# Softmax of a decode step that takes off each head's maximum: one exp per group of four heads

## The chip, the cores and the metric

The kernel runs on one core of one Trainium2 chip. The metric is the device time of one execution in microseconds (us); the time before is the median of three runs. A profile of one further execution shows each engine's instructions: TensorE (PE; its weight loads are PEld), VectorE (DVE), ScalarE (ACT), GpSimd (POOL) and SyncE (SP), which here only issues transfers and waits.

## The reference, cut to what matters

One token (batch 1, one query) goes through an attention block with a cached K and V and then through a gated MLP. All tensors are bf16. Layer norms have no weights.

```
q  = layernorm(x) @ wq                      # 640 -> 32 heads x 128
s  = q . k_cache * 128**-0.5                # per head 4096 scores
p  = softmax(s)                             # over the 4096 positions
o  = p . v_cache                            # per head 128 values
h  = x + o @ wo                             # 4096 -> 640
y  = layernorm(h)
out = h + (gelu(y @ w_gate) * (y @ w_up)) @ w_down     # 640 -> 1728 -> 640
```

K and V are 33.6 MB each (32 heads x 4096 positions x 128 values). Every byte of them is used once.

## The kernel before, in words

**Groups.** The 32 heads are worked off in 8 groups of four. A group's K (4.2 MB) is one transfer into one of three slots in SBUF, and so is its V. On the partitions, head j of the group has partitions 32j to 32j+31, and each partition holds 128 positions of that head, with their 128 values. The order of the transfers is K0 V0 K1 V1 ... K5 V5 K6 K7 V6 V7; the last V comes in two halves. Transfer n goes into slot n mod 3 and waits until what lay in it has been used: a K slot is free after the last of its four score multiplies, a V slot after its product (`consumed`, line 206). All of them, and the weights, are issued by SP in the order of the program (`issue`, line 197), so a transfer that waits holds up all behind it. After V7 come three parts of wo, which go into the arena that held wq, and then the MLP's weights (lines 462 to 468): two small parts of w_down, w_gate, w_up in two parts, four more parts of w_down. The first of these needs the slot of V7, so it waits for the product of group 7.

**Scores** (`scores`, line 416). A group's scores are made in four steps of 32 positions. DVE multiplies 128x4096 elements of K with the query (L295); PE folds the products eight-fold by matmuls with the identity (L305 and, for the repeated ones, the helper's line L28); DVE sums the remaining 16 (L313) into `sc`. `score_exp` (line 311) then has ACT make the exp of that step's 32 columns in four instructions (L317), one for each head's 32 partitions. Each writes into `p_bd`, in which position g has four columns, one per head: a head's partitions write only their own column, and the rest stays zero from a memset at the start. No maximum is taken off.

**Product with V** (`pv_group`, line 325). For every 8 positions PE takes 32 columns of `p_bd` as weights and multiplies them with two halves of V's 8 positions (L336, and L28 for the repeated weights). The result in `po` holds, beside wanted terms, those of other positions; DVE picks the wanted ones by a mask (`pick`, L353) and sums them (`pick_sum`, L363; for the last two groups three adds, L359 to L361) into `po_r`. PE then sums the 32 partitions of each head (`head_sum`, L369), four groups into one 16-row block of `ps_a`.

**Sums of the probabilities.** `p_sum` (line 348, L349) has DVE sum `p_bd` over the positions; after four groups `z_sum` (line 376) has PE sum over the partitions. `normalize` (line 380) takes the reciprocal and multiplies. `spread` and `take` turn the result into columns for the output projection, `proj_part` (line 395).

**Order.** Every engine works off its list in the order in which the program wrote it; only semaphores join the lists. Within `scores(G)` DVE's order is: multiplies and score sums alternately; before the last score sum the pick of the group whose product was written last (`run(first)`); after it that group's pick sum (`run(later)`); then the row sums of the group before. For K7 no pick is pending, so both lists are empty there. On PE the folds of K7 stand right ahead of the product of group 6.

**The end.** After the product of group 7 (lines 470 to 480): pick, pick sum, first half of the output projection, head sum, normalize, spread, take, second half. Then come the residual and the second layer norm, gate and up matmuls, GELU, the down projection and the output.

Of the kernel before, what the change touches and what calls it, by code (L numbers as in the profile page):

```python
# [17 lines left out]
INV_SQRT_DH = 1.0 / math.sqrt(DH)  # L18
GELU_C0 = math.sqrt(2.0 / math.pi)
GELU_C1 = 0.044715  # L20
NG = 8
# [88 lines left out]
def bass_sequential_preLN__gqa_block_cached__glu_gated_geglu__decode_kernel(nc, A_x, A_k_cache, A_v_cache, A_wq, A_wo, B_x, B_w_gate, B_w_up, B_w_down, out):  # L110
    sb = lambda name, shape, dt: nc.alloc_sbuf_tensor(name, shape, dt)
# [2 lines left out]
    arena = sb("arena", [128, 5 * 4096], BF16)  # L114
    prod = sb("prod", [128, 4, 32, DH], BF16)
    qb = sb("qb", [128, NG, DH], BF16)
    sc = sb("sc", [128, 4, 32], FP32)
    p_bd = sb("p_bd", [128, 2, 128, 4], BF16)
    RT = sb("RT", [128, H], FP32)
# [7 lines left out]
    hlnT = sb("hlnT", [128, 5], BF16)  # L127
    rz = sb("rz", [16, 2], FP32)
    po_m = sb("po_m", [128, 8, DH], FP32)
    po_r = sb("po_r", [128, 2, DH], FP32)  # L130
    m8_t = sb("m8_t", [128, 8, 4, 4], FP32)
    m8 = sb("m8", [128, 8], FP32)
    hs_t = sb("hs_t", [128, 4, 32], FP32)
    hs = sb("hs", [128, 28], FP32)
    aT = sb("aT", [16, 2, 128], BF16)
# [18 lines left out]
    ones_f = sb("ones_f", [128, 128], FP32)  # L154
# [14 lines left out]
    ps_d = bank[4][:, 256:416]  # L169
    ps_s = bank[5]  # L170
    ps_z = bank[6]
    ps_p = bank[7]
# [24 lines left out]
    def issue(upto):  # L197
        while state["next"] < min(upto, len(order)):
# [8 lines left out]
                         for i in range(parts)]  # L207
# [30 lines left out]
    c_par = GP(lambda e: e.affine_select(par_t[:, :, :], ones_b[:, 0:128].rearrange("p (a b) -> p a b", a=2),  # L238
                                         pattern=[[-1, 2], [-2, 64]], compare_op=ALU.is_equal,
                                         fill=0.0, base=0, channel_multiplier=1), c_onesb)  # L240
    c_pbd = GP(lambda e: e.memset(p_bd[:, :, :, :], 0.0))

    c_hs = V(lambda e: e.reduce_sum(hs[:, 12:16], hs_t[:, :, :], axis=AX.X), c_hs, c_hz)
    c_o4 = V(lambda e: e.reduce_max(ones4[:, :], sel4[:, :], axis=AX.X), c_s4)
    c_m8 = V(lambda e: e.reduce_sum(m8[:, :], m8_t[:, :, :, :].rearrange("p a b c -> p a (b c)"), axis=AX.X), c_m8)

    V(lambda e: e.reduce_sum(par[:, :], par_t[:, :, :], axis=AX.X), c_par)


    def x_cols(e):  # L250
# [35 lines left out]
    qc = A(lambda e: e.copy(qb[:, 4:8, :].rearrange("p g d -> p (g d)"), ps_q[1][:, :]), qd)  # L286


    folds, reds, exps, sums, pvs, evs, hds = {}, {}, {}, {}, {}, {}, {}

    def score_mult(s):
        G, n = s // 4, pos[("K", s // 4)]
# [15 lines left out]
            return i  # L308
        folds[s] = T(fold, m, c_idb, reds.get(s - 2))

    def score_exp(s):
        G = s // 4
        reds[s] = V(lambda e: e.reduce_sum(  # L313
            sc[:, s % 4, :], ps_f[s % 2][:, :].rearrange("p (g d) -> p g d", d=16), axis=AX.X),
            folds[s], exps.get(s - 4))
        for j in range(4):
            x = A(lambda e, j=j: e.activation(  # L317
                p_bd[32 * j:32 * j + 32, G % 2, 32 * (s % 4):32 * (s % 4) + 32, j],
                sc[32 * j:32 * j + 32, s % 4, :], ACTF.Exp,
                bias=zero_t[32 * j:32 * j + 32, 0:1], scale=INV_SQRT_DH),  # L320
                reds[s], pvs.get(G - 2), sums.get(G - 2), c_pbd, c_eps)
        exps[s] = x


    def pv_group(G):
        n = pos[("V", G)]
        vt = view(n)
        parts = len(landed[n])

        def pv_mm(e, c, half, load):  # L330
            a = 32 * (c % 4)
            args = (po[a:a + 32, 512 * half:512 * half + 512],
                    p_bd[:, G % 2, 8 * c:8 * c + 8, :].rearrange("p g j -> p (g j)"),
                    vt[:, 8 * c + 4 * half:8 * c + 4 * half + 4, :])
            if load:
                return e.matmul(*args, start=(c < 4), stop=(c >= 12))  # L336
            return matmul_again(nc, *args, c < 4, c >= 12, (128, 32), (0, a))

        for k in range(parts):
            def pv(e, k=k):  # L340
                for c4 in range(4 // parts * k, 4 // parts * (k + 1)):
                    for half in range(2):
                        for c in range(4 * c4, 4 * c4 + 4):
                            i = pv_mm(e, c, half, half == 0)
                return i
            pvs[G] = consumed[n] = T(pv, exps[4 * G + 3], landed[n][k], mks.get(G - 1))

    def p_sum(G):
        sums[G] = V(lambda e: e.reduce_sum(RT[:, 4 * G:4 * G + 4], p_bd[:, G % 2, :, :].rearrange("p g j -> p j g"), axis=AX.X),  # L349
                    exps[4 * G + 3])  # L350

    def pick(G):
        mks[G] = V(lambda e: e.tensor_tensor(  # L353
# [3 lines left out]
    def pick_sum(G):  # L357
        if G >= NG - 2:
            a1 = V(lambda e: e.tensor_add(po_m[:, 0:4, :], po_m[:, 0:4, :], po_m[:, 4:8, :]), mks[G])  # L359
            a2 = V(lambda e: e.tensor_add(po_m[:, 0:2, :], po_m[:, 0:2, :], po_m[:, 2:4, :]), a1)  # L360
            evs[G] = V(lambda e: e.tensor_add(po_r[:, G % 2, :], po_m[:, 0, :], po_m[:, 1, :]), a2, hds.get(G - 2))  # L361
            return
        evs[G] = V(lambda e: e.reduce_sum(po_r[:, G % 2, :], po_m[:, :, :].rearrange("p b d -> p d b"), axis=AX.X),  # L363
                   mks[G], hds.get(G - 2))
# [9 lines left out]
    mks, zs, z4s, spr, aPs = {}, {}, {}, {}, {}  # L374

    def z_sum(t):
        zs[t] = T(lambda e: e.matmul(ps_z[0:16, 0:1], RT[:, 16 * t:16 * t + 16], ones_f[:, 0:1], start=True, stop=True),
                  sums[4 * t + 3], aPs.get(t - 1))
# [49 lines left out]
    headed = 0  # L428
    for kind, G in order:
        if kind == "K":  # L430
            scores(G)
            continue
        run(first)
        run(later)
        pv_group(G)
        while headed in evs:
            head_sum(headed)
            headed += 1
        first.append(lambda G=G: pick(G))
        later.append(lambda G=G: pick_sum(G))  # L440
        if G == 4:
            z_sum(0)
# [159 lines left out]
```

## Time and profile before

| what | us |
|---|---|
| median of 3 runs (203.06 to 203.13) | 203.12 |
| the profiled execution | 202.97 |
| its span | 201.7 |
| DVE busy | 129.5 |
| PE busy | 115.3 |
| ACT busy | 51.3 |
| the costliest group: DVE multiply L295, 32 of 2283 ns | 72.4 |
| ACT exp L317, 128 of 362 ns | 46.4 |
| DVE score sum L313, 32 of 687 ns | 22.0 |
| DVE row sum L349, 8 of 675 ns | 5.4 |

The span is the time from the first to the last recorded instruction; what the device needs ahead of and behind it makes the profiled execution's time. A group line of the profile gives the line of the program, the engine, the operation and the shapes; then its busy time and the mean of one, then the idle time of the engine just before these instructions and what ended it. A line of the timeline gives the start and the length in us, the engine, the instructions merged into it, and in brackets the idle time before it and what ended that.

### The profile page before, as it was taken

The numbers are of one execution on the slowest core, as the hardware profiler recorded it, in microseconds if no ns is written. First come the engines' busy times: TensorE is split into PE (matmuls) and PEld (weight loads), VectorE is DVE, ScalarE is ACT, GpSimd is POOL, SyncE is SP. The second block draws the span as 40 slices with busy tenths as digits, with TensorE's granted clock in tenths as the row PEclk, the third lists the DMA queues.
The fourth block names the chain that finished last, engine by engine and source line by source line (L and its number), as shares of the span: only waits on it lengthen the run. The fifth ranks groups of instructions, "written<-read, shape, count | busy, mean of one in ns | idle before, by whom it ended". The sixth has DMA issues, their size and how long they took to land.

```text
span 201.7 us, 1568 instructions
## 1 busy us (share of the span) xinstructions
PE 115.3 (57%) x788; PEld 17.0 (8%) x384; DVE 129.5 (64%) x136; ACT 51.3 (25%) x139; POOL 5.6 (3%) x15
## 2 busy tenths in 40 slices
PE   0108059536737775197529655876396097754564
PEld 0101000000001000000000001001000000121222
DVE  1300188517994898379857966896879979683341
ACT  2100003610560055005502440252025214500111
POOL 7300000000000000000000000000000000000000
PEclk9999756996996699859997978798569859997575
DMA  9999999999999999999999999999999999999992
GB/s 333 439 398 455 442 422 416 416 442 468 432 422 416 416 422 455 443 442 417 416 416 445 442 448 422 422 416 429 442 442 448 387 429 423 427 409 439 415 408 99
DMA packets 4330, 84.32 MB, mean 418 GB/s; under 512 B 482, under 2 KB 868, under 8 KB 1508
## 3 DMA queue, kind: packets, MB, share of 16 engines
q1 hardware_dynamic: 4322, 84.23, 97.9%
q8 instruction: 4, 0.07, 0.1%
q14 instruction: 2, 0.02, 0.0%
q10 hardware_dynamic: 2, 0.00, 0.0%
HBM read 84.23 MB, written 0.00 MB: 418 GB/s over the span
## 4 chain that ended last, share of the span: by engine, by line
DMA 52%; DVE 21%; PE 19%; issue 3%; ACT 2%; SPq 2%
DMA slot<-in_A_k_cache_dram 43%; DVE prod L295 16%; PE bank L28 13%; DMA slot<-in_B_w_down_dram 9%; DVE sc L313 3%; PE bank L336 3%; PE bank L305 2%; ACT p_bd L317 2%; SPq L59 2%; DVE po_r L363 1%; DVE po_m L353 1%; PE bank L553 0%; DVE out_row L566 0%; DVE RT L349 0%; DVE aP L393 0%
## 5 line engine op out<-in xcount | busy, mean ns | idle before, releaser
L295 DVE TENSOR_TENSOR prod<-slot,qb 128x4096 bf16<-128x4096 bf16 x32 | 72.4, 2283 | 24.3 <-DMA slot<-in_A_k_cache_dram 24.3
L317 ACT ACTIVATE p_bd<-sc,zero_t 32x32 bf16<-32x32 f32 x128 | 46.4, 362 | 107.7 <-DVE sc L313 106.5
L28 PE MATMUL bank<-prod,id_b 128*128 128x512 bf16 x224 | 68.6, 458 | 0.0
L305 PE MATMUL bank<-prod,id_b 128*128 128x512 bf16 x32 | 15.3, 477 | 45.2 <-DVE prod L295 45.1
L313 DVE TENSOR_REDUCE sc<-bank 128x32 f32<-128x512 f32 x32 | 22.0, 687 | 14.7 <-PE bank L28 14.7
L336 PE MATMUL bank<-slot,p_bd 128*32 128x512 bf16 x128 | 14.8, 448 | 15.0 <-ACT p_bd L317 13.8
L28 PE MATMUL bank<-slot,p_bd 128*32 128x512 bf16 x128 | 14.9, 453 | 0.0
L305 PEld LDWEIGHTS bank<-prod,id_b 128*128 128x128 bf16 x32 | 3.5, 109 | 108.6 <-DVE prod L295 108.6
L363 DVE TENSOR_REDUCE po_r<-po_m 128x128 f32<-128x1024 f32 x6 | 11.2, 1867 | 0.0
L353 DVE TENSOR_TENSOR po_m<-bank,m 128x1024 f32<-128x1024 f32 x8 | 9.7, 1214 | 0.6 <-PE bank L28 0.6
L280 PE MATMUL bank<-arena,xlnB 128*32 128x512 bf16 x20 | 3.3, 628 | 7.2 <-DMA arena<-in_A_wq_dram 7.2
L285 DVE CAST qb<-bank 128x512 bf16<-128x512 f32 x1 | 0.7, 692 | 10.0 <-PE bank L28 10.0
L336 PEld LDWEIGHTS bank<-slot,p_bd 128*32 128x32 bf16 x128 | 3.8, 106 | 35.7 <-ACT p_bd L317 26.1
L509 PE MATMUL bank<-slot,hlnT 128*1 128x512 bf16 (+1 forms) x40 | 4.0, 486 | 2.7 <-DVE hX L500 2.2
L349 DVE TENSOR_REDUCE RT<-p_bd 128x4 f32<-128x512 bf16 x8 | 5.4, 675 | 0.0
L252 PE MATMUL bank<-one_bf,x_row 1*128 1x1 bf16 x5 | 0.4, 177 | 7.1 <-DMA x_row<-in_A_x_dram 7.1
L369 PE MATMUL bank<-po_r,hs 128*16 128x128 f32 x16 | 3.4, 301 | 1.5 <-DVE po_r L361 1.5
L286 ACT CAST qb<-bank 128x512 bf16<-128x512 f32 x1 | 0.6, 586 | 10.4 <-PE bank L28 10.4
L28 PE MATMUL bank<-arena,xlnB 128*32 128x512 bf16 x20 | 3.2, 613 | 0.0
L404 PE MATMUL bank<-arena,aP 128*1 128x320 bf16 x32 | 2.5, 314 | 1.1 <-DMA arena<-in_A_wo_dram 1.1
L263 ACT ACTIVATE ln<-ln,eps_t 128x1 f32<-128x1 f32 x2 | 0.6, 294 | 9.4 <-DVE ln L261 9.4
L482 ACT CAST A_hi<-bank 97x320 bf16<-97x320 f32 x1 | 0.4, 426 | 9.8 <-PE bank L28 9.8
(87 smaller groups left out, 42.9 us busy)
## 6 DMA issues: line engine op xcount, KB each, us to landing
slot<-in_A_k_cache_dram SPq DMA_DIRECT2D x8, 4096.0 KB, 21.0
slot<-in_A_v_cache_dram SPq DMA_DIRECT2D x7, 4096.0 KB, 17.7
arena<-in_A_wq_dram SPq DMA_DIRECT2D x1, 5120.0 KB, 15.5
slot<-in_A_v_cache_dram SPq DMA_DIRECT2D x2, 2048.0 KB, 14.9
arena<-in_A_wo_dram SPq DMA_DIRECT2D x1, 2560.0 KB, 22.9
slot<-in_B_w_gate_dram SPq DMA_DIRECT2D x1, 2160.0 KB, 11.0
arena<-in_A_wo_dram SPq DMA_DIRECT2D x1, 1920.0 KB, 27.0
slot<-in_B_w_up_dram SPq DMA_DIRECT2D x1, 1296.0 KB, 13.7
```

Source lines behind the costliest of these rows:

```text
L28: return e.add_instruction(mybir.InstMatmult(name=nc.get_next_instruction_name(), engine=e.engine, start_tensor_calc=start, stop_tensor_ca ...
L59: ev = self.op(eng, lambda e: e.dma_start(out, in_), *deps, dma=True)
L295: m = V(lambda e: e.tensor_tensor(out=prod[:, s % 4, :, :], in0=kt[:, 32 * u:32 * u + 32, :], in1=qb[:, G, :].unsqueeze(1).to_broadcast([1 ...
L305: i = e.matmul(*args, start=True, stop=False)
L313: reds[s] = V(lambda e: e.reduce_sum(sc[:, s % 4, :], ps_f[s % 2][:, :].rearrange("p (g d) -> p g d", d=16), axis=AX.X), folds[s], exps.ge ...
L317: x = A(lambda e, j=j: e.activation(p_bd[32 * j:32 * j + 32, G % 2, 32 * (s % 4):32 * (s % 4) + 32, j], sc[32 * j:32 * j + 32, s % 4, :], ...
L336: return e.matmul(*args, start=(c < 4), stop=(c >= 12))
L349: sums[G] = V(lambda e: e.reduce_sum(RT[:, 4 * G:4 * G + 4], p_bd[:, G % 2, :, :].rearrange("p g j -> p j g"), axis=AX.X), exps[4 * G + 3])
L353: mks[G] = V(lambda e: e.tensor_tensor(out=po_m[:, :, :], in0=po[:, :].rearrange("p (b d) -> p b d", b=8), in1=m8[:, :].unsqueeze(2).to_br ...
L363: evs[G] = V(lambda e: e.reduce_sum(po_r[:, G % 2, :], po_m[:, :, :].rearrange("p b d -> p d b"), axis=AX.X), mks[G], hds.get(G - 2))
L369: return e.matmul(ps_a[0:16, 128 * (G // 4):128 * (G // 4) + 128], hs[:, 12 - 4 * g:28 - 4 * g], po_r[:, G % 2, :], start=(g == 0), stop=( ...
L509: i = e.matmul(po[32 * a:32 * a + 1, 512 * k:512 * k + n], hlnT[:, c:c + 1], w[:, c, 512 * a:512 * a + n], start=(c == 0), stop=(c == 4))
```

## The change

The exp no longer runs step by step. `score_sum` only makes the four score sums, into a doubled `sc`. When a group's last is done, `head_max` takes each partition's maximum (DVE), writes it on the diagonal of 32 columns (ACT, a copy of `d32` with the maximum as scale), and PE multiplies that with `blk`, which is -1/sqrt(128) within each head's 32 partitions and zero elsewhere: 32 columns in which every partition sees the negated, scaled maxima of its head's 32 partitions. `exp_group` takes the minimum of these (DVE), makes one exp of 128x128 with it as the bias (ACT), whose row sums go into an extra column of `po_r`, and spreads the result into `p_bd` by a multiply with the head mask (DVE), zeros included. `pv_group` waits for that spread. The row sums now pass through `head_sum`, which has 129 columns for 128; `p_sum` and `z_sum` are gone, and `normalize` takes its reciprocal from the head sums. `po_r` has four buffers for two. At the start the zeroing of `p_bd` on POOL makes way for one mask there, and two small instructions on DVE are added.

```diff
@@ buffers @@
-    sc = sb("sc", [128, 4, 32], FP32)
+    sc = sb("sc", [128, 2, 4, 32], FP32)
+    mx = sb("mx", [128, NG], FP32)
+    mxd = sb("mxd", [128, 32], FP32)
+    nb = sb("nb", [128, NG], FP32)
+    p_t = sb("p_t", [128, 2, 128], BF16)
...
-    po_r = sb("po_r", [128, 2, DH], FP32)
+    po_r = sb("po_r", [128, 4, DH + 1], FP32)
@@ start @@
-    c_pbd = GP(lambda e: e.memset(p_bd[:, :, :, :], 0.0))
+    c_d32 = GP(lambda e: e.affine_select(d32_t[:, :, :], ones_f[:, :].rearrange("p (a b) -> p a b", a=4),
+                                         pattern=[[-32, 4], [-1, 32]], compare_op=ALU.is_equal,
+                                         fill=0.0, base=0, channel_multiplier=1), c_ones)
...
+    c_d32 = V(lambda e: e.reduce_sum(d32[:, :], d32_t[:, :, :].rearrange("p a n -> p n a"), axis=AX.X), c_d32)
+    c_blk = V(lambda e: e.tensor_scalar(blk[:, :, :], hs[:, 12:16].unsqueeze(2).to_broadcast([128, 4, 32]),
+                                        -INV_SQRT_DH, None, ALU.mult), c_hs)
@@ scores @@
-    def score_exp(s):
-        G = s // 4
+    def score_sum(s):
         reds[s] = V(lambda e: e.reduce_sum(
-            sc[:, s % 4, :], ps_f[s % 2][:, :].rearrange("p (g d) -> p g d", d=16), axis=AX.X),
-            folds[s], exps.get(s - 4))
-        for j in range(4):
-            x = A(lambda e, j=j: e.activation(
-                p_bd[32 * j:32 * j + 32, G % 2, 32 * (s % 4):32 * (s % 4) + 32, j],
-                sc[32 * j:32 * j + 32, s % 4, :], ACTF.Exp,
-                bias=zero_t[32 * j:32 * j + 32, 0:1], scale=INV_SQRT_DH),
-                reds[s], pvs.get(G - 2), sums.get(G - 2), c_pbd, c_eps)
-        exps[s] = x
+            sc[:, (s // 4) % 2, s % 4, :], ps_f[s % 2][:, :].rearrange("p (g d) -> p g d", d=16), axis=AX.X),
+            folds[s], exps.get(s // 4 - 2))
+
+    def head_max(G):
+        m = V(lambda e: e.reduce_max(mx[:, G:G + 1], sc[:, G % 2, :, :].rearrange("p u g -> p (u g)"), axis=AX.X), reds[4 * G + 3])
+        d = A(lambda e: e.activation(mxd[:, :], d32[:, :], ACTF.Copy, scale=mx[:, G:G + 1]), m, c_d32, mxs.get(G - 1))
+        mxs[G] = T(lambda e: e.matmul(ps_s[:, 64:96], blk[:, :, :].rearrange("p a b -> p (a b)"), mxd[:, :], start=True, stop=True),
+                   d, c_blk, nbs.get(G - 1))
+
+    def exp_group(G):
+        nbs[G] = V(lambda e: e.tensor_reduce(nb[:, G:G + 1], ps_s[:, 64:96], AX.X, ALU.min), mxs[G])
+        exps[G] = A(lambda e: e.activation(
+            p_t[:, G % 2, :], sc[:, G % 2, :, :].rearrange("p u g -> p (u g)"), ACTF.Exp, bias=nb[:, G:G + 1],
+            scale=INV_SQRT_DH, accum_out=po_r[:, G % 4, DH:DH + 1]), nbs[G], pbs.get(G - 2), hds.get(G - 4))
+        pbs[G] = V(lambda e: e.tensor_tensor(
+            out=p_bd[:, G % 2, :, :], in0=p_t[:, G % 2, :].unsqueeze(2).to_broadcast([128, 128, 4]),
+            in1=hs[:, 12:16].unsqueeze(1).to_broadcast([128, 128, 4]), op=ALU.mult), exps[G], pvs.get(G - 2), c_hs)
@@ product, sums, normalization @@
-            pvs[G] = consumed[n] = T(pv, exps[4 * G + 3], landed[n][k], mks.get(G - 1))
-
-    def p_sum(G):
-        sums[G] = V(lambda e: e.reduce_sum(RT[:, 4 * G:4 * G + 4], p_bd[:, G % 2, :, :].rearrange("p g j -> p j g"), axis=AX.X),
-                    exps[4 * G + 3])
+            pvs[G] = consumed[n] = T(pv, pbs[G], landed[n][k], mks.get(G - 1))
...
-            return e.matmul(ps_a[0:16, 128 * (G // 4):128 * (G // 4) + 128], hs[:, 12 - 4 * g:28 - 4 * g],
-                            po_r[:, G % 2, :], start=(g == 0), stop=(g == 3))
-        hds[G] = T(fn, evs[G], z4s.get(G // 4 - 1), c_hs, qa, qc)
...
-        rc = V(lambda e: e.reciprocal(rz[:, t:t + 1], ps_z[0:16, 0:1]), zs[t])
-        z4s[t] = V(lambda e: e.tensor_scalar(aT[:, t, :], ps_a[0:16, 128 * t:128 * t + 128], rz[:, t:t + 1], None, ALU.mult),
-                   rc, hds[4 * t + 3])
+            return e.matmul(ps_a[0:16, 132 * (G // 4):132 * (G // 4) + DH + 1], hs[:, 12 - 4 * g:28 - 4 * g],
+                            po_r[:, G % 4, :], start=(g == 0), stop=(g == 3))
+        hds[G] = T(fn, evs[G], exps[G], z4s.get(G // 4 - 1), c_hs, qa, qc)
...
+        rc = V(lambda e: e.reciprocal(rz[:, t:t + 1], ps_a[0:16, 132 * t + DH:132 * t + DH + 1]), hds[4 * t + 3])
+        z4s[t] = V(lambda e: e.tensor_scalar(aT[:, t, :], ps_a[0:16, 132 * t:132 * t + DH], rz[:, t:t + 1], None, ALU.mult), rc)
@@ order within scores(G) @@
         for i in range(4):
             score_mult(4 * G + i)
             if i >= 1:
-                score_exp(4 * G + i - 1)
+                score_sum(4 * G + i - 1)
         run(first)
-        score_exp(4 * G + 3)
+        score_sum(4 * G + 3)
+        head_max(G)
         run(later)
-        if G > 0:
-            p_sum(G - 1)
+        exp_group(G)
         issue(pos[("K", G)] + 1 + NSLOT)
...
-    p_sum(NG - 1)
     pick(NG - 1)
     pick_sum(NG - 1)
     proj_part(0, 0, 16, aPs[0], d_wo["0"], reds[4 * NG - 1])
-    z_sum(1)
     head_sum(NG - 1)
     normalize(1)
```

More of the change, by code (lines that the diff above doesn't have):

```diff
@@ L116, in bass_sequential_preLN__gqa_block_cached__glu_gated_geglu__decode_kernel @@
     qb = sb("qb", [128, NG, DH], BF16)
-    sc = sb("sc", [128, 4, 32], FP32)
+    sc = sb("sc", [128, 2, 4, 32], FP32)
[3 more added lines that the diff above has]
+    p_t = sb("p_t", [128, 2, 128], BF16)
+    d32_t = sb("d32_t", [128, 4, 32], FP32)
+    d32 = sb("d32", [128, 32], FP32)
+    blk = sb("blk", [128, 4, 32], FP32)
     p_bd = sb("p_bd", [128, 2, 128, 4], BF16)
-    RT = sb("RT", [128, H], FP32)
     x_row = sb("x_row", [1, D], BF16)
@@ L168, in bass_sequential_preLN__gqa_block_cached__glu_gated_geglu__decode_kernel @@
     ps_a = bank[4]
-    ps_d = bank[4][:, 256:416]
+    ps_d = bank[4][:, 264:424]
     ps_s = bank[5]
@@ L286, in bass_sequential_preLN__gqa_block_cached__glu_gated_geglu__decode_kernel @@
     qc = A(lambda e: e.copy(qb[:, 4:8, :].rearrange("p g d -> p (g d)"), ps_q[1][:, :]), qd)
-    folds, reds, exps, sums, pvs, evs, hds = {}, {}, {}, {}, {}, {}, {}
+    folds, reds, exps, pbs, pvs, evs, hds = {}, {}, {}, {}, {}, {}, {}
     def score_mult(s):
@@ L360, in pick_sum @@
             a2 = V(lambda e: e.tensor_add(po_m[:, 0:2, :], po_m[:, 0:2, :], po_m[:, 2:4, :]), a1)
-            evs[G] = V(lambda e: e.tensor_add(po_r[:, G % 2, :], po_m[:, 0, :], po_m[:, 1, :]), a2, hds.get(G - 2))
+            evs[G] = V(lambda e: e.tensor_add(po_r[:, G % 4, 0:DH], po_m[:, 0, :], po_m[:, 1, :]), a2, hds.get(G - 4))
             return
-        evs[G] = V(lambda e: e.reduce_sum(po_r[:, G % 2, :], po_m[:, :, :].rearrange("p b d -> p d b"), axis=AX.X),
-                   mks[G], hds.get(G - 2))
+        evs[G] = V(lambda e: e.reduce_sum(po_r[:, G % 4, 0:DH], po_m[:, :, :].rearrange("p b d -> p d b"), axis=AX.X),
+                   mks[G], hds.get(G - 4))
     def head_sum(G):
@@ L368, in fn @@
             g = G % 4
-            return e.matmul(ps_a[0:16, 128 * (G // 4):128 * (G // 4) + 128], hs[:, 12 - 4 * g:28 - 4 * g],
-                            po_r[:, G % 2, :], start=(g == 0), stop=(g == 3))
-        hds[G] = T(fn, evs[G], z4s.get(G // 4 - 1), c_hs, qa, qc)
[L374 to L378, printed above, removed]
+            return e.matmul(ps_a[0:16, 132 * (G // 4):132 * (G // 4) + DH + 1], hs[:, 12 - 4 * g:28 - 4 * g],
+                            po_r[:, G % 4, :], start=(g == 0), stop=(g == 3))
+        hds[G] = T(fn, evs[G], exps[G], z4s.get(G // 4 - 1), c_hs, qa, qc)
+    mks, z4s, spr, aPs, mxs, nbs = {}, {}, {}, {}, {}, {}
     def normalize(t):
-        rc = V(lambda e: e.reciprocal(rz[:, t:t + 1], ps_z[0:16, 0:1]), zs[t])
-        z4s[t] = V(lambda e: e.tensor_scalar(aT[:, t, :], ps_a[0:16, 128 * t:128 * t + 128], rz[:, t:t + 1], None, ALU.mult),
-                   rc, hds[4 * t + 3])
+        rc = V(lambda e: e.reciprocal(rz[:, t:t + 1], ps_a[0:16, 132 * t + DH:132 * t + DH + 1]), hds[4 * t + 3])
+        z4s[t] = V(lambda e: e.tensor_scalar(aT[:, t, :], ps_a[0:16, 132 * t:132 * t + DH], rz[:, t:t + 1], None, ALU.mult), rc)
     def spread(t):
@@ L441, in bass_sequential_preLN__gqa_block_cached__glu_gated_geglu__decode_kernel @@
         if G == 4:
-            z_sum(0)
             later.append(lambda: normalize(0))
```

## The prediction

> **What bounds the kernel now.** I read the page first: busy shares, slices, queues.
>
> ```profile
> span 201.7 us, 1568 instructions
> PE 115.3 (57%) x788; PEld 17.0 (8%) x384; DVE 129.5 (64%) x136; ACT 51.3 (25%) x139; POOL 5.6 (3%) x15
> ...
> DMA  9999999999999999999999999999999999999992
> ...
> q1 hardware_dynamic: 4322, 84.23, 97.9%
> ```
>
> No engine is full, while one queue of transfers is busy for 97.9% of the span and has no gap before the last slice. 84.23 MB over 201.7 us is the 418 GB/s of the page. So an operation costs time only if it makes a transfer start late, or if it stands behind the last transfers. The waits of VectorE (DVE) give the room in the loop over groups:
>
> ```profile
> DVE prod L295 <- DMA slot<-in_A_k_cache_dram: 24.3, 7, 5.0
> ...
> DVE sc L313 <- PE bank L28: 14.7, 16, 1.5
> ```
>
> Seven of the eight groups begin with DVE idle for its K transfer; the timeline gives 2.65 to 4.98 us each. Only K7 does not: DVE reaches it late. That stretch, in the timeline, is where I look next:
>
> ```profile
> 155.75 0.69 DVE L313 TENSOR_REDUCE sc<-bank 128x32 f32<-128x512 f32 x1 [0.27 <-PE bank L28]
> 156.36 1.86 DVE L363 TENSOR_REDUCE po_r<-po_m 128x128 f32<-128x1024 f32 x1
> ...
> 158.22 0.68 DVE L349 TENSOR_REDUCE RT<-p_bd 128x4 f32<-128x512 bf16 x1
> 158.81 4.48 DVE L295 TENSOR_TENSOR prod<-slot,qb 128x4096 bf16<-128x4096 bf16 x2
> ...
> 172.35 0.40 PE L336 MATMUL bank<-slot,p_bd 128*32 128x512 bf16 x4
> 172.46 0.69 DVE L313 TENSOR_REDUCE sc<-bank 128x32 f32<-128x512 f32 x1 [1.39 <-PE bank L28]
> ...
> 174.31 1.23 DVE L353 TENSOR_TENSOR po_m<-bank,m 128x1024 f32<-128x1024 f32 x1 [0.56 <-PE bank L28]
> ...
> 175.68 0.40 PE L336 MATMUL bank<-slot,p_bd 128*32 128x512 bf16 x4 [1.20 <-DVE po_m L353]
> ...
> 177.62 0.81 SPq L59 DMA_DIRECT2D slot<-in_B_w_down_dram  x2
> ```
>
> Here nothing waits for a transfer: K7's scores, the probability-times-V product of group 6 (pv 6), its pick (L353), then pv 7. The end of pv 7, 177.60, releases the slot that the last eight weight transfers wait for. Last, the tail:
>
> ```profile
> 182.26 0.31 PE L404 MATMUL bank<-arena,aP 128*1 128x320 bf16 x4 [0.59 <-DMA arena<-in_A_wo_dram]
> ...
> 183.77 0.43 PE L404 MATMUL bank<-arena,aP 128*1 128x320 bf16 x4 [0.53 <-DMA arena<-in_A_wo_dram]
> ...
> 194.76 0.60 PE L509 MATMUL bank<-slot,hlnT 128*1 128x512 bf16 x8 [0.48 <-DMA slot<-in_B_w_up_dram]
> ...
> 197.95 0.70 PE L553 MATMUL bank<-slot,hm 128*1 128x160 bf16 x16 [0.30 <-DMA slot<-in_B_w_down_dram]
> ...
> 199.10 0.70 PE L553 MATMUL bank<-slot,hm 128*1 128x160 bf16 x16 [0.45 <-DMA slot<-in_B_w_down_dram]
> ```
>
> From pv 7 on, TensorE (PE) and the transfers run side by side, and PE waits for a transfer five times, for 0.3 to 0.6 us. These waits are all the room there is.
>
> **The change, part by part.**
>
> *ScalarE (ACT).* Per group 16 exps of 362 ns go (46.4 us in all). One exp of 128x128 and one 128x32 copy come. The 128x14 exp (L541) takes 307 ns, and from a 160- to a 512-column copy (286 to 586 ns) a column costs 0.85 ns, so the exp is 0.40 us and the copy 0.32. Nothing waits for ACT's load as such, so the 40 us saved are worth nothing. The exp's second output, its row sum, has no row: between nothing and one more short ACT instruction (294 ns, L263); I take nothing, as no row shows ACT needing two, and keep 0.3 for the range.
>
> *DVE.* Eight 675 ns row sums go. Per group come a maximum over 128x128 (288 ns, the row of L243), a minimum over 32 columns of PSUM (168 ns for 10 columns, L260, so about 0.19) and the masked spread to 512 columns (692 ns, L359, same size, two operands; its stride could cost or save at most what separates it from L349's 675, so no more than 0.02). Busy time grows by 8 x 0.5 = 4 us. The setup's two DVE instructions and one on GpSimd lie before 25.25 us, where DVE idles 4.50 us for K0.
>
> *The new chain, loop groups.* DVE is in order, so it now stands still while ACT makes the exp. Counting from the start of the group's last score sum (155.75 for group 6): max 0.72 to 1.01; the sum of the picks (1.87, and the 0.16 copy for group 6) to 2.88; the maximum's way over ACT and PE (0.04+0.32, then 0.69 as from L258's end to L260's start) is ready at 2.07, hidden under it; minimum to 2.99; exp 3.03 to 3.43; spread 3.47 to 4.16; next multiply at 4.09. Before, it came 158.81 - 155.75 = 3.06 after. So +1.03 us per group. Six times that falls into DVE's idle time of at least 2.65 us: no cost. pv starts some 1.9 us later too, and with it SP's issue for the slot it frees, with every later transfer of that in-order queue behind it; but the K issue at 81.50 was landed only at 103.24, behind a V of 9.7 us (half of the 19.4 between the K landings) that began when K3 landed at 83.86, so it had over 10 us to spare: no cost. Without that cover each group would pay its 1.03.
>
> *K6 to K7.* No idle time here: **+1.03**.
>
> *K7 to pick 6.* No pick sum covers the maximum's way now, and its matmul stands ahead of pv 6 in PE's in-order queue. From the last score sum's start: max done 1.01, copy 1.05 to 1.37, matmul 1.40 to 2.00 (L259: 0.60), pv 6 then takes its 1.93 (172.35 to 174.28) to 3.96, pick at 3.99. DVE's own minimum, exp and spread end at 3.43, within that. Before, the pick came 174.31 - 172.46 = 1.85 after. **+2.14**. pv 7 keeps its distance to pick 6, so it ends **3.17 us later**, at 180.77.
>
> *Weights.* The eight transfers are issued from about 180.8. Is the stream still busy? The 2 us windows from 182 to 199 add up to 6.7 MB; the weights behind the output projection's are 6.6 MB, so the stream runs dry near 182.2, and the first three issues bring the large one 0.85 us later. From issue to first byte has no row; an output write of 1.2 KB takes 1.1 us in all, the first x row, behind other transfers, 5.8. Nearest is the output write. I take 1: the stream just stays fed, with a gap of at most some tenths, and the range keeps a gap of 3. [...]
>
> *Tail.* Pick 7, its sums and the head sum follow pv 7 as before (+3.17). The reciprocal, earlier done ahead, now needs the head sum: +0.18 (147 ns and a handoff). The second row sum at 176.96 and its PE product vanish, both in the cover of pv 7. So the output projection can start at 185.3 instead of 182.26. Its two waits are gone: 0.98 + 0.70 us of work less 0.2 overlap end at 186.8, before 184.47: +2.3. The gate matmuls start 2.3 later (the gate weights landed at 189.5, in time); the second up part loses its 0.48 wait: +1.8. The down projection starts at 198.7; before, its 2.91 us held 0.75 of waiting and up to 0.45 of pipeline overlap that waiting broke, so the end moves by 1.8 - 0.75 to 1.8 - 1.2, that is **+0.6 to +1.05; I take +0.8**. The last transfer landed by 199.5, before this work's end at 200.6, so even a gap of one microsecond would not add.
>
> *Sum.* 202.97 us (the profiled execution, span 201.7 and 1.3 around it) + 0.8 = 203.8. It lies 0.15 below the median of the three runs, 203.12; against that the forecast is **203.9 us**. The tail absorbs some 2.4 of the 3.35 us.
>
> **The rivals.**
>
> *A. Not slower: the tail absorbs it all.* Two of K7's folds run at half clock (matmul starts 0.43 us apart, later 0.21), and DVE waits 1.49 us for the first; K6 shows the same 1.49. Group 2 took 12.9 us from landing to its last score sum, group 6 13.7: the clock's timing is worth up to 0.8 per group, 1.5 in two. It need only save 0.4 (pv 7 at most 2.8 us later) for the end to stay within 0.4 us: then **203.1 to 203.4**. Against it: of groups 1 to 6, five took 13.1 or more.
>
> *B. A slow clock in pv 6.* PE now idles some 1.4 us ahead of the new matmul and little runs until pv 6. After a gap of 2.30 us, pv 1 and pv 4 ran at half clock (3.4 us, pv 2 took 1.95). That adds 1.5 us to pv 7's end and, the tail having no room left, to the time: **205.4**. Against it: pv 7 itself ran at full clock after a gap of 1.2 us. [...]
>
> *C. The weights come late.* If a transfer needs 3 us from issue to its first byte, the stream stands still for about 1.5; its end, 199.5 + 1.5, and the two waits it puts back into the down projection end **about 0.6 beyond** the forecast, 204.5. For it: the margin above is a few tenths. Against: the 1.1 us write.
>
> *D. Faster.* Lighter ACT and DVE traffic would have to speed the stream. For it: slices vary from 387 to 468 GB/s; 0.5% would give **202.1**. Against: the slices do not follow ACT's busy times.
>
> The limit of what a measurement of this kernel can tell from no change is about 0.2%, 0.4 us.
>
> **How the numbers follow.** Forecast (203.5 to 204.6 with its own costs, the row sum's 0.3 included) 0.47, A 0.24, B 0.18, C 0.06, D 0.05. Slower by over 0.2%: forecast, B and C, 0.71; within: most of A, 0.23; faster: D and a little of A, 0.06. The range from 203.0 (most of A) to 205.5 (B) leaves out D, a cold pv 7 on top of B and A's lower edge: under 2 in 10.
>
> **What would show it.** In the new profile: VectorE still idle for K in seven groups, by about 1 us less; K7's first multiply about 1 us later; pv 6 behind the new small matmul, not against the last fold; the first w_down issue near 180.8; no PE wait for the output-projection weights, and the down matmuls running without waits to about 200.6. If instead the first w_down issue comes before 180, A holds; with pv 6 over 3 us long, B; if the windows from 182 show the transfers idle, C. A main loop in which DVE no longer waits for K would make the whole reading wrong.

## The result, and the profile after

The changed kernel takes 203.53 us (median of 22 executions, 202.95 to 205.45) against 203.11 of the kernel before (22 executions, 202.92 to 203.51). The medians differ by 0.42 us, the means by 0.64 (ratio 1.0033, interval 1.0021 to 1.0046). It is slower, by about as little as can be told. The median hides two kinds of execution: 11 of the 22 lie at 203.38 or below, like the kernel before; seven at 203.7 to 204.3; one at 204.74, three at 205.05 to 205.45. A repeat (e8 below) had a median of 203.14, with four of twelve executions above 204.4, so the median follows the share of long executions. The profiled execution is of the first kind: 202.95 us, span 201.7, as long as the one before.

Its page, busy shares, slices, queue and the groups that are new:

```profile
span 201.7 us, 1476 instructions
PE 115.9 (57%) x800; PEld 19.5 (10%) x396; DVE 133.9 (66%) x154; ACT 11.4 (6%) x35; POOL 5.0 (2%) x15
...
DMA  9999999999999999999999999999999999999992
...
q1 hardware_dynamic: 4322, 84.23, 97.8%
...
L338 DVE TENSOR_TENSOR p_bd<-p_t,hs 128x512 bf16<-128x512 bf16 x8 | 5.5, 692 | 4.5 <-ACT p_t L335 4.5
...
L335 ACT ACTIVATE p_t<-sc,nb 128x128 bf16<-128x128 f32 x8 | 3.2, 401 | 11.3 <-DVE nb L334 11.3
```

ACT lost 40 us of work, DVE gained 4.4, and the queue is as full as before. DVE's waits:

```profile
DVE prod L306 <- DMA slot<-in_A_k_cache_dram: 19.4, 7, 4.4
DVE sc L323 <- PE bank L28: 10.4, 14, 1.5
...
DVE p_bd L338 <- ACT p_t L335: 4.5, 8, 0.6
```

Seven groups still begin with DVE idle for K, 4.9 us less in all than before (24.3), and DVE stands still 0.56 us per group for the exp.

The timeline from the product of group 5 (pv 5) to the first late weight transfer:

```profile
139.83 0.62 PE L354 MATMUL bank<-slot,p_bd 128*32 128x512 bf16 x4 [2.81 <-DVE p_bd L338]
...
142.24 4.50 DVE L306 TENSOR_TENSOR prod<-slot,qb 128x4096 bf16<-128x4096 bf16 x2 [2.46 <-DMA slot<-in_A_k_cache_dram]
...
144.59 0.39 PE L316 MATMUL bank<-prod,id_b 128*128 128x512 bf16 x1 [0.76 <-DVE prod L306]
...
154.33 0.69 DVE L323 TENSOR_REDUCE sc<-bank 128x32 f32<-128x512 f32 x1 [0.26 <-PE bank L28]
155.05 0.29 DVE L328 TENSOR_REDUCE mx<-sc 128x1 f32<-128x128 f32 x1
155.25 1.87 DVE L377 TENSOR_REDUCE po_r<-po_m 128x128 f32<-128x1024 f32 x1
157.12 0.18 DVE L334 TENSOR_REDUCE nb<-bank 128x1 f32<-128x32 f32 x1
157.34 0.40 ACT L335 ACTIVATE p_t<-sc,nb 128x128 bf16<-128x128 f32 x1 [1.64 <-DVE nb L334]
...
157.64 0.19 ACT L335 ACTIVATION_READ_ACCUMULATOR p_t<-sc,nb 128x1 f32 x1
157.86 0.69 DVE L338 TENSOR_TENSOR p_bd<-p_t,hs 128x512 bf16<-128x512 bf16 x1 [0.56 <-ACT p_t L335]
158.47 4.49 DVE L306 TENSOR_TENSOR prod<-slot,qb 128x4096 bf16<-128x4096 bf16 x2
...
171.78 0.69 DVE L323 TENSOR_REDUCE sc<-bank 128x32 f32<-128x512 f32 x1 [1.40 <-PE bank L28]
...
173.20 0.41 PE L330 MATMUL bank<-mxd,blk 128*128 128x32 f32 x2 [1.46 <-ACT mxd L329]
...
175.49 1.22 DVE L367 TENSOR_TENSOR po_m<-bank,m 128x1024 f32<-128x1024 f32 x1 [0.40 <-PE bank L28]
...
178.71 0.80 SPq L59 DMA_DIRECT2D slot<-in_B_w_down_dram  x2
```

The new chain is there, step for step, and so is its price. Yet the first late weight transfer is issued 1.09 us after that of before (177.62), not the forecast 3.17. One stage paid most of the difference, 1.58 of 2.08 us: from K6's first multiply to its last score sum it is 154.33 - 142.24 = 12.09 us, where before it was 155.75 - 142.08 = 13.67. A second profile of the same kernel (e10_look) has the stage at its old length. The three side by side, in us:

| step | before | changed | changed, e10_look |
|---|---|---|---|
| K6's first multiply starts | 142.08 | +0.16 | +0.31 |
| K6's stage, to its last score sum | 13.67 | -1.58 | -0.01 |
| from there to K7's first multiply | 3.06 | +1.08 | +1.08 |
| K7's stage, to its last score sum | 13.65 | -0.34 | -0.31 |
| from there to pick 6 | 1.85 | +1.86 | +1.86 |
| from there to the first weight issue | 3.31 | -0.09 | -0.09 |
| first weight issue | 177.62 | +1.09 | +2.84 |
| span | 201.7 | 0.0 | +0.8 |

The added work costs the same in both; K6's stage makes the difference. The product of group 5 and the first fold of K6, in the kernel before:

```profile
138.08 0.40 PE L336 MATMUL bank<-slot,p_bd 128*32 128x512 bf16 x4 [2.30 <-ACT p_bd L317]
...
144.43 0.61 PE L305 MATMUL bank<-prod,id_b 128*128 128x512 bf16 x1 [3.11 <-DVE prod L295]
```

In these stretches a matmul of this size takes 0.39 or 0.40 us where the granted clock is 1.00 and 0.61 to 0.66 where it is 0.50, but for those during which it changes. So in the changed kernel pv 5 starts 1.75 us later and at half clock (0.62), and K6's first fold runs at full clock (0.39); before, pv 5 started at full clock (0.40) and the fold ran at half (0.61).

The tail of the short execution looks like that of before:

```profile
194.76 0.60 PE L515 MATMUL bank<-slot,hlnT 128*1 128x512 bf16 x8 [0.26 <-DMA slot<-in_B_w_up_dram]
...
199.08 0.70 PE L559 MATMUL bank<-slot,hm 128*1 128x160 bf16 x16 [0.43 <-DMA slot<-in_B_w_down_dram]
```

The last w_down matmuls wait for their transfer as before (0.43 us at 199.08; before 0.45 at 199.10).

### The profile page after: what moved, and what is told of

Read it like the earlier page. It is cut to its first block, busy times and chain, and to the rows that moved or that the text cites. A ratio compares the mean times of both kernels' runs of the same rounds, so it can differ in the third digit from the quotient of the medians.

```text
span 201.7 us, 1476 instructions
## 1 busy us (share of the span) xinstructions
PE 115.9 (57%) x800; PEld 19.5 (10%) x396; DVE 133.9 (66%) x154; ACT 11.4 (6%) x35; POOL 5.0 (2%) x15
## 4 chain that ended last, share of the span: by engine, by line
DMA 48%; DVE 29%; PE 19%; SPq 2%; issue 1%; ACT 1%
DMA slot<-in_A_k_cache_dram 40%; DVE prod L306 18%; PE bank L28 12%; DMA slot<-in_B_w_down_dram 8%; DVE sc L323 5%; PE bank L354 4%; DVE po_r L377 3%; PE bank L316 2%; SPq L59 2%; DVE p_bd L338 1%; DVE mx L328 1%; DVE po_m L367 1%; ACT p_t L335 0%; PE bank L330 0%; PE bank L559 0%
## 5 line engine op out<-in xcount | busy, mean ns | idle before, releaser
L306 DVE TENSOR_TENSOR prod<-slot,qb 128x4096 bf16<-128x4096 bf16 x32 | 72.5, 2285 | 19.4 <-DMA slot<-in_A_k_cache_dram 19.4
L28 PE MATMUL bank<-prod,id_b 128*128 128x512 bf16 x224 | 60.0, 413 | 0.0
L316 PE MATMUL bank<-prod,id_b 128*128 128x512 bf16 x32 | 14.0, 437 | 34.4 <-DVE prod L306 34.3
L323 DVE TENSOR_REDUCE sc<-bank 128x32 f32<-128x512 f32 x32 | 22.0, 687 | 10.4 <-PE bank L28 10.4
L354 PE MATMUL bank<-slot,p_bd 128*32 128x512 bf16 x128 | 18.2, 558 | 14.9 <-DVE p_bd L338 13.8
L28 PE MATMUL bank<-slot,p_bd 128*32 128x512 bf16 x128 | 18.3, 559 | 0.0
L329 ACT ACTIVATE mxd<-d,mx 128x32 f32<-128x32 f32 x8 | 2.6, 322 | 136.2 <-DVE mx L328 136.2
L330 PE MATMUL bank<-mxd,blk 128*128 128x32 f32 x16 | 3.3, 286 | 11.7 <-ACT mxd L329 11.7
L338 DVE TENSOR_TENSOR p_bd<-p_t,hs 128x512 bf16<-128x512 bf16 x8 | 5.5, 692 | 4.5 <-ACT p_t L335 4.5
L354 PEld LDWEIGHTS bank<-slot,p_bd 128*32 128x32 bf16 x128 | 4.4, 125 | 27.1 <-DVE p_bd L338 14.5
L383 PE MATMUL bank<-po_r,hs 128*16 128x129 f32 x16 | 4.1, 348 | 1.5 <-DVE po_r L375 1.5
L330 PEld LDWEIGHTS bank<-mxd,blk 128*128 128x128 f32 x16 | 2.4, 188 | 26.1 <-ACT mxd L329 26.1
L335 ACT ACTIVATE p_t<-sc,nb 128x128 bf16<-128x128 f32 x8 | 3.2, 401 | 11.3 <-DVE nb L334 11.3
## 6 DMA issues: line engine op xcount, KB each, us to landing
arena<-in_A_wo_dram SPq DMA_DIRECT2D x1, 2560.0 KB, 24.3
```

The lines of the kernel that those rows point to most:

```text
L28: return e.add_instruction(mybir.InstMatmult(name=nc.get_next_instruction_name(), engine=e.engine, start_tensor_calc=start, stop_tensor_ca ...
L306: m = V(lambda e: e.tensor_tensor(out=prod[:, s % 4, :, :], in0=kt[:, 32 * u:32 * u + 32, :], in1=qb[:, G, :].unsqueeze(1).to_broadcast([1 ...
L316: i = e.matmul(*args, start=True, stop=False)
L323: reds[s] = V(lambda e: e.reduce_sum(sc[:, (s // 4) % 2, s % 4, :], ps_f[s % 2][:, :].rearrange("p (g d) -> p g d", d=16), axis=AX.X), fol ...
L330: mxs[G] = T(lambda e: e.matmul(ps_s[:, 64:96], blk[:, :, :].rearrange("p a b -> p (a b)"), mxd[:, :], start=True, stop=True), d, c_blk, n ...
L338: pbs[G] = V(lambda e: e.tensor_tensor(out=p_bd[:, G % 2, :, :], in0=p_t[:, G % 2, :].unsqueeze(2).to_broadcast([128, 128, 4]), in1=hs[:, ...
```

## The experiments

e1, e2, e3 and e8 ran on one chip, the other runs on a second; each ratio is against the kernel before on the same chip (medians 203.11 and 203.07 us).

My theory: only the chain of groups 6 and 7 costs, since the loop's waits for K hide the rest; what varies from execution to execution is the clock at which K6's and K7's folds run. The rivals: the loop's additions cost too, through V's issue times; or the weights' transfers, not the tail's compute, set the end.

**e1_nomax_67: the maximum left out in groups 6 and 7.**

```diff
-        nbs[G] = V(lambda e: e.tensor_reduce(nb[:, G:G + 1], ps_s[:, 64:96], AX.X, ALU.min), mxs[G])
+        with_max = G < 6
+        if with_max:
+            nbs[G] = V(lambda e: e.tensor_reduce(nb[:, G:G + 1], ps_s[:, 64:96], AX.X, ALU.min), mxs[G])
...
-        head_max(G)
+        if G < 6:
+            head_max(G)
```

Without the maximum the exp's bias is zero.

> The changed kernel, but groups 6 and 7 take no maximum off (bias zero, no small matmul); groups 0 to 5 do. Theory (the loop hides everything, the price arises between K6 and pv 7): K7's multiply begins about 0.35 us later than in the kernel before, pick 6 at most 0.1 more, so pv 7 ends about 0.5 us late, well inside the tail's 2.4: 203.0 to 203.2, with no execution above 203.6. Rival (the first six groups' chain or their slower products cost something): it stays at the changed kernel's 203.5, with executions up to 205.

Measured: 203.21 us (202.88 to 203.32), ratio 1.0004 (0.9996 to 1.0013). The whole loss is gone, and so is the scatter: no span is above 202.1 us, where ten of the changed kernel's 22 are 202.4 or longer. Six groups with the full chain cost no time. The first weight issue came at 176.18, 1.4 us ahead of that of before, where I had expected it some 0.5 later: K6's stage was short here too (12.09 us).

**e2_max_67_only: the reverse, `if G >= 6`.**

> The changed kernel, but only groups 6 and 7 take the maximum off; groups 0 to 5 have bias zero and no small matmul. Theory: as the changed kernel, median 203.4 to 204, executions up to 205. Rival (the price is in the first six groups): 203.0 to 203.2 with little scatter.

Measured: 204.74 us (203.97 to 205.05), ratio 1.0076 (1.0060 to 1.0092). With less work than the changed kernel its median is 1.2 us longer; neither side expected that. The timeline, the end of pv 5 (SP's issue that it releases) and the first fold of K6:

```profile
140.35 0.33 SPq L59 DMA_DIRECT2D slot<-in_A_v_cache_dram  x1
...
144.53 0.61 PE L316 MATMUL bank<-prod,id_b 128*128 128x512 bf16 x1 [3.71 <-DVE prod L306]
...
180.58 0.80 SPq L59 DMA_DIRECT2D slot<-in_B_w_down_dram  x2
```

Without the loop's maximum pv 5 ends at 140.35, PE idles 3.71 us, and the folds start at half clock (0.61 us a matmul for 0.39): K6's stage is 13.67 us. In the changed kernel pv 5 starts late, ends at 143.37, and the gap is 0.76. So the delay of pv, which I had called free, can shorten the stage behind it. The kept traces bear this out: with a gap of 3.1 us or more (before, e2, e3) K6's first fold was at half clock in three of three; with 1.9 or less at full clock in eight of ten (e9, with matmuls in the gap, is not counted). K7's first fold, after gaps of 3.4 to 5.5 us, was at half clock in 13 of 13, all but e6. The two exceptions in K6 are e5 and e10_look, the latter with a gap like the changed kernel's:

```profile
144.74 0.61 PE L316 MATMUL bank<-prod,id_b 128*128 128x512 bf16 x1 [0.71 <-DVE prod L306]
...
180.46 0.80 SPq L59 DMA_DIRECT2D slot<-in_B_w_down_dram  x2
```

The granted clock in the traces tells the two kinds apart. In the traces of the kernel before and of the changed kernel each two changes in a row lie 3.41 us or a multiple of it apart, and the grid that they make lies 0.45 us later in the second than in the first. Around pv 5 the clock is at half in the changed kernel from 139.7 to 143.1, a step that the late pv 5 fills with work (3.26 of 3.41 us), and K6's folds, from 144.6, find the full clock. In e10 the grid lies 1.65 us earlier; PE works 1.75 and 2.71 us of the first two steps, and half clock lasts from 138.0 to 148.3. In the kernel before, where pv 5 is over early, it lasts from 139.2 to 149.5. Where half clock ended before K6's first fold the stage took 12.09 us, but for e4, where it came back (12.81), and e9 with its matmuls in the way (13.62); where it ended at 145.4 and 145.9 (e11, e5) 12.48 and 12.78; at 148.3 and later 13.66 and 13.67. The full clock followed a step that PE filled for 3.26 us (changed kernel) and one of 3.41 (before, to 149.5); steps of 1.75 and 2.71 us (e10) and of 2.10 and 1.63 (before) were followed by half clock. No run varies this alone. Nor is the maximum needed to narrow the gap: in e4, whose code is that of before up to there, pv 5 ran at half clock (0.62 us a matmul), and the gap was 1.86 us.

**e3_before_wait2, e4_before_wait4: the kernel before, with two or four dummy additions of 1.23 us on DVE ahead of pick 6.**

```diff
     def pick(G):
+        dl = evs.get(G - 1)
+        for _ in range(2 if G == 6 else 0):
+            dl = V(lambda e: e.tensor_add(po_m[:, :, :], po_m[:, :, :], po_m[:, :, :]), dl)
...
```

> The kernel before, with two additions of 128x1024 on VectorE (about 1.25 us each, into a buffer that is free then) ahead of the pick of group 6. Pick 6 and pv 7 come about 2.0 us later. Theory (the tail has room for 2.4 to 2.5): 203.0 to 203.3, no change. Rival (no such room, or the weights' transfers come late at once): 204 to 205.

> The kernel before, with four additions of 128x1024 on VectorE (about 1.25 us each) ahead of the pick of group 6: pick 6 and pv 7 come about 4.5 us later. Theory (room of 2.5, then one for one): +2.0, 205.1. Rival (transfers bind: a long time from issue to first byte): a gap of more than 1 us in the weights' stream, and 206 or more. Rival (more room than thought): under 204.

Measured: e3 204.48 us (203.83 to 204.98), ratio 1.0067 (1.0050 to 1.0083); e4 207.11 (206.64 to 207.62), 1.0204 (1.0187 to 1.0221). Both times the theory missed, and the rival that the transfers bind held. In e3 pick 6 was 2.2 us late, but the first weight issue 3.5:

```profile
177.87 0.62 PE L336 MATMUL bank<-slot,p_bd 128*32 128x512 bf16 x4 [3.14 <-DVE po_m L356]
...
181.11 0.81 SPq L59 DMA_DIRECT2D slot<-in_B_w_down_dram  x2
...
200.93 0.70 PE L556 MATMUL bank<-slot,hm 128*1 128x160 bf16 x16 [0.46 <-DMA slot<-in_B_w_down_dram]
```

After 3.14 us of idling PE made pv 7 at half clock, which my "no change" had left out; and at the end it still waited for the last w_down transfer. e4 shows why. The view by windows of 1 us: the columns are busy time and number of instructions of PE, PEld, DVE, ACT and POOL, then the clock, the transfers' share and GB/s. Its weights are issued from 183.11:

```profile
181.00:182.00 1.00, 1.00 (x13) 0.18 (x4) 0.43 (x1) 0.00 (x0) 0.00 (x0) 0.50 0.65 266
182.00:183.00 1.00, 1.00 (x16) 0.30 (x5) 0.00 (x0) 0.00 (x0) 0.00 (x0) 0.50 0.25 102
183.00:184.00 1.00, 1.00 (x37) 0.53 (x13) 0.89 (x1) 0.00 (x0) 0.00 (x0) 0.97 0.01 5
184.00:185.00 1.00, 0.45 (x12) 0.19 (x2) 0.96 (x2) 0.00 (x0) 0.00 (x0) 1.00 0.78 230
185.00:186.00 1.00, 0.10 (x1) 0.10 (x2) 0.85 (x4) 0.00 (x0) 0.00 (x0) 1.00 1.11 258
186.00:187.00 1.00, 0.50 (x10) 0.22 (x9) 0.34 (x1) 0.00 (x0) 0.00 (x0) 1.00 0.83 294
187.00:188.00 1.00, 0.73 (x27) 0.33 (x15) 0.17 (x1) 0.00 (x0) 0.00 (x0) 1.00 0.92 363
```

The stream does not stop at once at 182.2, as the prediction had it from even rates: it thins out from 181 on (266, 102 and 5 GB/s against a mean of 418), which loses 2.1 us of stream by 184. The first bytes come about 1 us after the issue (nothing until 184.0), and from 184 to 188 the rate only climbs back to 363 GB/s, which loses another 1.3. The slow rise (1.3 us) costs no less than the wait for the first byte (about 1). Where the queue still has transfers nothing of the kind is seen: in the kernel before, the windows from 182 to 184 carry 502 and 431 GB/s, and the first of these weights, 80 KB, is down at about 184.4, 6.4 us after its issue.

e10_look, where the issue came at 180.46, shows the same in small:

```profile
181.00:182.00 1.00, 0.72 (x18) 0.11 (x4) 0.97 (x2) 0.00 (x0) 0.00 (x0) 1.00 0.90 325
182.00:183.00 1.00, 0.00 (x0) 0.00 (x0) 0.93 (x3) 0.00 (x0) 0.00 (x0) 1.00 1.22 360
183.00:184.00 1.00, 0.39 (x2) 0.11 (x2) 0.48 (x3) 0.00 (x0) 0.00 (x0) 1.00 0.96 326
184.00:185.00 1.00, 0.46 (x12) 0.35 (x12) 0.39 (x2) 0.00 (x0) 0.00 (x0) 1.00 0.75 312
```

These four add up to 1323 where the mean of 418 makes 1672: a loss of 0.83 us of stream, and the span is 0.8 longer. The short execution of the changed kernel (issue 178.71) has 369, 511, 447 and 397 there: no loss. Taking such a loss over all windows from 180 to 197 for each trace:

| kernel | first weight issue | loss of stream, us | span |
|---|---|---|---|
| e1 | 176.18 | 0.06 | 201.8 |
| before | 177.62 | 0.10 | 201.7 |
| e7 | 177.77 | 0.06 | 201.8 |
| e6 | 177.80 | 0.07 | 202.0 |
| changed | 178.71 | 0.09 | 201.7 |
| changed, e8 | 178.71 | 0.09 | 201.8 |
| changed, e12 | 179.24 | 0.11 | 201.7 |
| e5 | 179.57 | 0.31 | 203.5 |
| changed, e11 | 179.73 | 0.27 | 202.0 |
| changed, e10 | 180.46 | 0.79 | 202.5 |
| e2 | 180.58 | 1.03 | 202.8 |
| e9 | 180.73 | 0.99 | 202.6 |
| e3 | 181.11 | 1.43 | 203.5 |
| e4 | 183.11 | 3.43 | 205.6 |

Up to an issue at about 179.5 nothing is lost; beyond about 179.8 every microsecond of delay is one of lost stream, and but for e5 the span follows within 0.6 us. So the room is 179.8 - 177.6 = 2.2 us, and the transfers set it. The point fits the trace of e4: an issue at 179.8 brings its first bytes at about 180.8, just before the stream thins out.

**e5_after_loop1: the changed kernel with one such addition ahead of the picks of groups 1 to 4.**

> The changed kernel with one more addition of 128x1024 on VectorE (1.25 us) in each of groups 2 to 5, ahead of the pick there: the loop's added VectorE time is more than doubled. Theory: VectorE's idle time ahead of K shrinks by 1.25 per group and the time stays that of the changed kernel (203.0 to 204). Rival (the loop has no room left): +1 or more per group, 206 or more.

Measured: 203.27 us (202.94 to 205.0), ratio 1.0027 (1.0006 to 1.0048), as the changed kernel without it. DVE's wait for K falls from 19.4 to 17.4 us, not by the 5 expected; its wait for the folds fell beside it, from 10.4 to 8.3:

```profile
DVE prod L306 <- DMA slot<-in_A_k_cache_dram: 17.4, 7, 4.6
...
DVE sc L323 <- PE bank L28: 8.3, 8, 1.5
```

The loop has room for more than the change used. The profiled execution was a long one, 205.0 us, and is the outlier of the table: its span of 203.5 is not explained by its stream's loss of 0.31. Its second part of w_up landed 3.7 us after the first, before 2.06, and PE waited 1.53 us for it; why is open.

**e6_warm: the changed kernel with 20 matmuls without use, eight ahead of K7's stage, eight more once group 6's exp is done, four before its last score sum.** They fill PE's idle time there.

```diff
+        if G == NG - 1:
+            warm(8)
+            warm(8, exps[6])
...
+        if G == NG - 1:
+            warm(4)
```

> The changed kernel with 20 extra matmuls of 128x512 on TensorE into an unused bank: 8 behind the small matmul of group 6, 8 behind its exp, 4 between K7's last fold and its small matmul, where TensorE idles. They change no result. Theory (the clock's timing in K7's folds and pv 6 makes the scatter): K7's folds run at full clock, K7's stage takes about 12.5 instead of 13.3 to 13.7 us, and the median falls toward 203.1 with fewer executions above 204. Rival (clock not the cause): median and scatter as the changed kernel's.

Measured: 203.07 us (202.80 to 203.26), ratio 0.9999 (0.9991 to 1.0008). K7's first fold in the changed kernel:

```profile
160.81 0.61 PE L316 MATMUL bank<-prod,id_b 128*128 128x512 bf16 x1 [4.66 <-DVE prod L306]
```

and in e6:

```profile
161.12 0.39 PE L316 MATMUL bank<-prod,id_b 128*128 128x512 bf16 x1 [1.03 <-DVE prod L306]
```

K7's stage falls from 13.31 to 12.09 us, the issue comes at 177.80, and no execution lies above 203.3. This shows that half-clock folds are worth 1.2 us in that stage. With that margin the scatter is gone: none of the eleven spans is above 202.0 us, where on the same chip three of e5's ten are 202.5 or longer.

**e7_defer6: group 6's spread moved behind K7's first multiply.**

```diff
             score_mult(4 * G + i)
+            if G == 7 and i == 0:
+                spread_group(6)
```

> The changed kernel, but group 6's spread is put behind K7's first multiply on VectorE, which so no longer stands still for group 6's exp. K7's first multiply starts about 1.2 us earlier than in the changed kernel, the fourth score sum about 0.5 earlier. Theory: pv 7 ends about 0.5 us earlier; the median falls by 0.1 to 0.4. Rival (that standing still is hidden anyway by K7's waits for folds): no change.

Measured: 203.09 us (202.94 to 203.74), ratio 1.0005 (0.9996 to 1.0014); K7's multiply starts at 157.18, the issue comes at 177.77. A microsecond off the chain takes the loss away too: no span is above 202.1 us, and the one execution at 203.74 has a span of 201.8.

**e8_after_again, e10_look, e11_look, e12_look: the changed kernel, unchanged.**

> The changed kernel once more, unchanged, for a second profile. Theory: its time hangs on when pv 7 ends; 203.0 where the folds of K6 and K7 and pv 6 find the full clock, 204 where the first weight transfer is issued near 180.8, 205 where pv 6 or pv 7 runs at half clock over 3 us. Rival (the scatter comes from the transfers themselves): single times differ at the same end of pv 7.

> The changed kernel unchanged, one look, to find an execution of the longer kind. Theory: an execution with a span of 202.8 to 203.6 shows K6's or K7's first folds, pv 6 or pv 7 at half clock, and a first weight transfer issued after 179.4; one with 201.7 to 202.1 shows it issued before. Rival: a long span with an early issue.

> The same look a second time: theory and rival as for the first.

> The same look a third time: theory and rival as for the first.

Measured: e8 203.14 us (202.84 to 205.59), ratio 1.0028 (1.0003 to 1.0053). Profiled: e8 203.27 us with K6's stage at 12.09; e12 202.94 with 12.09; e11 203.21 with 12.48; e10 203.75 with 13.66. A later issue goes with a longer span; in e12 it is K7's stage that makes it later than in e8 (13.79 against 13.39 us). None of them shows the product of group 6 at half clock (its matmuls take 0.39 or 0.40 us).

**e9_max67_warm6: e2 with 12 matmuls without use ahead of K6's first fold.**

> The kernel with the maximum in groups 6 and 7 only, with 12 extra matmuls of 128x512 into an unused bank on TensorE between the product of group 5 and K6's first fold; they change no result. Theory (that kernel is slower than the full change because the product of group 5 ends early, TensorE idles some 4 us and K6's first folds run at half clock): K6's stage falls from 13.7 to about 12.1 us, the first weight transfer is issued near 179, the median falls from 204.7 to 203.1 to 203.8. Rival (another cause in the groups without a maximum): it stays at 204.5 or more.

Measured: 204.36 us (203.04 to 205.36), ratio 1.0060 (1.0036 to 1.0083). It decides little: in the profiled execution pv 5 began at half clock (0.62 us a matmul), and the fillers stood in the way until K6's first fold at 146.38 (e2: 144.53); the stage took 13.62. Four of twelve executions were at 203.52 or below, which e2 (on the other chip, six executions) never was. That a warm PE alone would cure e2 was not shown.

## Why the prediction was right, and where it was not

- **What bounds the kernel, and where the change costs.** Right: e1 and e5 show the loop's additions free, and DVE still waits for K in seven groups.
- **K6 to K7, +1.03.** Measured +1.08, in both executions. The exp's second output, taken as nothing with 0.3 in the range, is a second ACT instruction of 186 ns, of which 0.09 us lie beyond the exp's end; DVE's spread starts 0.03 us behind it.
- **K7 to pick 6, +2.14.** Measured +1.86. Most of the difference is the small matmul: it took 0.41 us at full clock, where I had taken 0.60 from L259, which ran at half clock (granted 0.50 at 186.8).
- **"pv starts some 1.9 us later: no cost."** This step failed, by its sign. I followed the late pv into SP's queue and found cover there, but not into PE's own idle time. It started 1.75 us later and, at half clock, ended 2.7 later, and so closed the gap ahead of K6's folds, which then mostly run at full clock: 1.58 us gained, half of the 3.17 that I had pv 7 late. This is rival A's mechanism, in K6, and by the prediction's own sign (an issue before 180) the kept profile, 178.71, speaks for A, and e10, 180.46, for the forecast. Of five profiled executions of the changed kernel K6's stage was short in three, nearly so in one and long in one; that it decides between short and long in the others is inferred. Where it fails (e10), my chain holds within 0.33 us: 2.84 for 3.17.
- **"The stream just stays fed", one microsecond from issue to first byte.** The microsecond is right (e4: issue at 183.11, nothing until 184.0). But the stream thins out before it stops (266 and 102 GB/s) and recovers slowly (1.3 us lost by 188): loss begins at an issue of 179.8, 2.4 us ahead of the 182.2 at which I had it run dry, not 1.0. That is what rival C claimed, to which I had given 0.06, but not by its cause, a first byte after 3 us.
- **Tail: compute sets the end, the down matmuls run without waits, +0.8.** The cause was wrong, and that the size was right is luck. In e10 the span is 0.8 longer, as much as the stream lost (0.83 us), and PE still waits for the last transfer, longer than before:

```profile
199.88 0.70 PE L559 MATMUL bank<-slot,hm 128*1 128x160 bf16 x16 [0.72 <-DMA slot<-in_B_w_down_dram]
```

- **Rival B**, pv 6 at half clock, is in no trace of the changed kernel (its matmuls take 0.39 or 0.40 us in all five). Half clock did hit pv 7, in e3 and e4 (0.62 us), after idling of 3.14 and 5.66 us.
- **The time.** 203.9 was a figure of the longer kind of execution; the median of 203.53 lies between two kinds that I had written as alternatives and that alternate. That it came so near is luck in part: the executions with K6's gain, which I had not seen, did not get longer, and in e10, without it, the +0.8 goes with lost stream and not with the tail's work. What makes the few executions at 205 and above is open. In some of them about a microsecond lies outside the span (205.17 us with a span of 202.8; usually the two differ by 1.2 to 1.35); no trace of such an execution was kept.

## What to carry to other kernels

When work moves later on an engine whose clock is seen to change with what it does (K7's first fold took 0.61 us in the changed kernel and 0.39 behind e6's added matmuls), look at the idle time that it leaves and closes there as well as at the queues: here a delay of pv paid for half of what the change added, in some of the executions. Give a queue of transfers its next one well before it would run dry at an even rate, here some 2.4 us: in e4 thinning out and refilling cost 2.1 and 1.3 us of stream, the first byte's delay about 1. And where a step lies near the edge of its room, take several profiles: one alone would have shown this change as free, another as 0.8 us.

## What the runs showed of the hardware

- In the traces of the kernel before and of the changed kernel the granted clock changed only on a grid of 3.41 us: each half-clock stretch but the last lasted one, two or three such steps (3.41, 6.83 or 10.24 us). The grid lay elsewhere in each execution (half clock around pv 5 from 139.2 in the kernel before, 139.7 in the changed kernel, 138.0 in e10), and K6's first fold, the same code with nearly the same gap ahead of it (0.76 and 0.71 us), ran at full clock in the changed kernel's first profile (0.39 us) and at half in e10 (0.61). The step ahead of a drop to half clock was not empty: PE was busy for 1.15 us of it in the kernel before (drop at 139.2), 0.41 in the changed kernel (139.7) and 1.02 in e3 (177.1).
- The queue, which got its next transfer only at 183.11, thinned out to 266 and 102 GB/s from 181 on before it stood still; after that it carried 230, 258, 294 and 363 GB/s in the first four microseconds, against 418 on average (e4).
- An exp of 128x128 whose row sums are also written takes 401 ns, and a second record of 186 ns reads the sums out; the consumer of the exp's main output started only behind that (changed kernel, group 6: 157.64 + 0.19, then 157.86).
